# Decode attention and gated MLP block on one Trainium2 core: heads 1 to 14 as a loop on the chip over standing buffers

## The chip, the core and the metric

The kernel runs on one core of a Trainium2 chip. A core has five engines with instruction streams of their own: TensorE (PE, matrix multiply into PSUM), VectorE (DVE), ScalarE (ACT), GpSimd (POOL) and SyncE (SP), which here only issues loads. Sixteen DMA engines move data between HBM and the on-chip memory (SBUF). The engines order each other by semaphores. The metric is the device time of one execution in microseconds; lower is better.

## The reference

One token for each of two batch rows passes a pre-norm attention block with a KV cache and then a bilinear gated MLP. All data are 32-bit floats.

```python
B, Sq, D = 2, 1, 448          # batch, one query token, model width
H, Sk, Dh = 16, 8192, 256     # heads, cached keys, head width; F = 1792
q = (layernorm(x) @ wq).reshape(B, Sq, H, Dh).transpose(0, 2, 1, 3)
scores = einsum("bhqd,bhkd->bhqk", q, k_cache) * Dh ** -0.5
o = einsum("bhqk,bhkd->bhqd", softmax(scores), v_cache)
h = x + o.transpose(0, 2, 1, 3).reshape(B, Sq, H * Dh) @ wo
n = layernorm(h)
out = h + ((n @ w_gate) * (n @ w_up)) @ w_down
```

Each of the 32 pairs of head and batch row reads 8 MB (8192 KB) of K and 8 MB of V once; this is nearly all of the data.

## The kernel before, in words

The work is one Python loop over steps n = 0 to 32 (lines 306 to 343), written out flat in the instruction streams; n counts pairs of head and batch row, h = n // 2, b = n % 2. Step n computes the scores of pair n and the weighted sum over V of pair n - 1, so K of one pair and V of the pair before are loaded together. The order of the instructions on each engine is the order of the code (`manual_schedule`).

A pair's K comes in two chunks of 4096 KB (`load_cache`, line 160): 128 partitions by 32 keys by 256. In `scores` (line 232) VectorE takes half a chunk at a time: a product with the query (line 239) into `prod`, and a reduction over the head width (line 242), so there are four products and four reductions to a pair. `top` (line 246) takes the maximum of each partition and TensorE transposes it. In the next step `softmax` (line 253) runs between the first and the second quarter of the scores, `norm` a quarter later, and `mix` (line 272) has TensorE multiply the probabilities with V, two keys at a time, into `o_ps`. `mixed` (line 283) gathers that into a column, scales it and, when both batch rows of a head are there, multiplies it with `wo` and adds it to `acc_ps`, which stays in PSUM for the whole kernel.

All loads of the cache and the weights are issued by SP, in the order of the code: for each chunk index first K, then V, and behind chunk 0 the weights of that step. SP waits in this order too: a load that must wait for its buffer holds up all that stand behind it. The buffers of the cache are a pool of four (`RING = 4`), handed out in turn to whichever chunk comes next, K or V. Step 0 has no V, so its two K chunks take buffers 0 and 1, and step 1's K and V chunks 0 take buffers 2 and 3; from step 1 on the order K, V, K, V comes round to the same four places. A K buffer is free when the second product over it has ended (line 239), a V buffer when the `mix` matmuls over it have ended (line 278).

The query weights come for two heads at once (`load_wq`, 896 KB, double buffered), one load in four steps; `queries` (line 206) makes four queries in one place, in the second step of an odd head, between the two halves of `mix`. `first_queries` (line 191) makes those of heads 0 and 1. The output weights `wo` come head by head (448 KB).

Behind step 32 come the MLP's three weight loads, which take ring buffers as they come free, the residual add (line 389), the second norm and the projections.

Of the kernel before, what the change touches and what calls it, by code (L numbers as in the profile page):

```python
# [24 lines left out]
RING = 4  # L25
WQ, WO = 3 * 2 * DH + DH, 2 * D
# [17 lines left out]
def tile_decode_block(  # L44
# [23 lines left out]
    ring = ctx.enter_context(tc.tile_pool(name="ring", bufs=RING))  # L68
    wpool = ctx.enter_context(tc.tile_pool(name="wpool", bufs=2))
    qpool = ctx.enter_context(tc.tile_pool(name="qpool", bufs=4))  # L70
    work = ctx.enter_context(tc.tile_pool(name="work", bufs=2))
    ps_q = ctx.enter_context(tc.tile_pool(name="ps_q", bufs=2, space=bass.MemoryType.PSUM))
    ps_s = ctx.enter_context(tc.tile_pool(name="ps_s", bufs=2, space=bass.MemoryType.PSUM))
    ps_1 = ctx.enter_context(tc.tile_pool(name="ps_1", bufs=1, space=bass.MemoryType.PSUM))
# [24 lines left out]
    o_ps = [ps_1.tile([P, 2 * DH], F32, name=f"o_ps{i}") for i in range(2)]  # L99
    for t in o_ps:  # L100
        nc.vector.memset(t, 0.0)  # L101
# [15 lines left out]
    def center(h, tag):  # L117

        mean = ps_s.tile([P, B], F32, tag="sm", name=f"mean_{tag}")
        nc.tensor.matmul(mean, avg, over_chunks(h, f"h_{tag}"), start=True, stop=True)  # L120
# [17 lines left out]
    def transposed(src, tag):  # L138
        ps = ps_s.tile([P, DC, B], F32, tag="sm", name=f"T_ps_{tag}")
        for c in range(DC):  # L140
            nc.tensor.transpose(ps[:, c, :], src[:, c * P : (c + 1) * P], ident[:B, :B])
# [4 lines left out]

    def load_wq(hp):
        t = wpool.tile([P, WQ], F32, tag="wq", name=f"wq_{hp}")
        nc.sync.dma_start(t, wq[hp])
# [4 lines left out]
    def load_wo(h):

        if h % 2 == 0:
            wo_t[h // 2] = wpool.tile([P, 2, WO], F32, tag="wo", name=f"wo_{h // 2}")
        nc.sync.dma_start(wo_t[h // 2][:, h % 2, :], wo[h])

    def load_cache(src, b, h, c, name, parts=(JC,)):  # L160
        t = ring.tile([P, JC, DH], F32, tag="ring", name=f"{name}_{h}_{b}_{c}")
        n = P * JC
        keys = src[b, h, c * n : (c + 1) * n].rearrange("(p j) d -> p j d", p=P)
        at = 0
        for k in parts:
            nc.sync.dma_start(t[:, at : at + k, :], keys[:, at : at + k, :])
# [10 lines left out]
    var = ps_s.tile([P, B], F32, tag="sm", name="var_x")  # L177
# [13 lines left out]
    def first_queries(w):  # L191

        got = [qpool.tile([P, 2, DH], F32, tag="q", name=f"q_0_{b}") for b in range(B)]
        for k in range(2):
            for b in range(B):
                ps = ps_q.tile([P, DH], F32, tag="q", name=f"q_ps_0_{k}_{b}")
                for c in range(DC):
                    at = c * 2 * DH + (k * DH if c < DC - 1 else 0)
                    nc.tensor.matmul(  # L199
                        ps, xb[:, c + (k if c == DC - 1 else 0), b, :], w[:, at : at + DH],  # L200
                        start=(c == 0), stop=(c == DC - 1),
                    )
                nc.scalar.activation(got[b][:, k, :], ps, AF.Copy)
        return got

    def queries(hp, w):

        got = []
        for b in range(B):
            ps = ps_q.tile([P, 2 * DH], F32, tag="q", name=f"q_ps_{hp}_{b}")  # L210
            for c in range(DC - 1):
                nc.tensor.matmul(  # L212
                    ps, xb[:, c, b, :], w[:, c * 2 * DH : (c + 1) * 2 * DH],
                    start=(c == 0), stop=False,
                )
            for k in range(2):
                nc.tensor.matmul(  # L217
                    ps[:, k * DH : (k + 1) * DH], xb[:, DC - 1 + k, b, :],
                    w[:, 3 * 2 * DH : WQ], start=False, stop=(k == 1),
                )  # L220
            q = qpool.tile([P, 2, DH], F32, tag="q", name=f"q_{hp}_{b}")
            nc.scalar.activation(q.rearrange("p h d -> p (h d)"), ps, AF.Copy)  # L222
            got.append(q)
        return got
# [4 lines left out]
    s_t, p_t, rl_t, l_t, mT_t, oT_t = {}, {}, {}, {}, {}, {}
    HC = JC // 2  # L230

    def scores(i, kt, part):
# [6 lines left out]
        nc.vector.tensor_mul(  # L239
            prod, kt[c][:, k * HC : (k + 1) * HC, :], q[:, None, :].to_broadcast([P, HC, DH])  # L240
        )
        nc.vector.tensor_reduce(  # L242
            s_t[i][:, part * HC : (part + 1) * HC], prod, axis=AX.X, op=ALU.add
        )

    def top(i):

        m = work.tile([P, 1], F32, tag="m", name=f"m_{i}")
        nc.vector.tensor_reduce(m, s_t[i], axis=AX.X, op=ALU.max)  # L249
        mT_t[i] = ps_s.tile([1, P], F32, tag="sm", name=f"mT_{i}")  # L250
        nc.tensor.transpose(mT_t[i], m, ident)  # L251

    def softmax(i):
        nm = work.tile([1, 1], F32, tag="nm", name=f"nm_{i}")
        nc.vector.tensor_reduce(nm, mT_t[i], axis=AX.X, op=ALU.max, negate=True)  # L255
        nb_ps = ps_s.tile([P, 1], F32, tag="sm", name=f"nb_ps_{i}")
        nc.tensor.matmul(nb_ps, row, nm, start=True, stop=True)  # L257
        nb = work.tile([P, 1], F32, tag="nb", name=f"nb_{i}")
        nc.scalar.activation(nb, nb_ps, AF.Copy)  # L259
        p_t[i] = work.tile([P, NJ], F32, tag="p", name=f"p_{i}")  # L260
        lsum = work.tile([P, 1], F32, tag="lsum", name=f"lsum_{i}")
# [4 lines left out]
        nc.tensor.matmul(l_t[i], ones, lsum, start=True, stop=True)  # L266

    def norm(i):
        rl_t[i] = work.tile([P, 1], F32, tag="rl", name=f"rl_{i}")
        nc.vector.reciprocal(rl_t[i], l_t[i])  # L270

    def mix(i, vt, c):

        o, p = o_ps[i % 2], p_t[i]
        for t in range(c * JC // 2, (c + 1) * JC // 2):
# [7 lines left out]
    def mixed(i):  # L283

        h, b = divmod(i, B)
        o_sb = work.tile([P, 2 * DH], F32, tag="o_sb", name=f"o_sb_{i}")
        nc.scalar.activation(o_sb, o_ps[i % 2], AF.Copy)  # L287
        oT_ps = ps_s.tile([P, 2], F32, tag="sm", name=f"oT_ps_{i}")
# [8 lines left out]
        nc.scalar.activation(oT_t[h][:, :, b], oT_ps, AF.Copy, scale=rl_t[i])  # L297
        if b == B - 1:
            w = wo_t[h // 2][:, h % 2, :]
            for c in range(2):  # L300
                nc.tensor.matmul(  # L301
                    acc_ps, oT_t[h][:, c, :], w[:, c * D : (c + 1) * D],
                    start=(h == 0 and c == 0), stop=(h == H - 1 and c == 1),
                )

    for n in range(NQ + 1):
        kt, vt = [], []
        hp, at = divmod(n, 2 * B)
        for c in range(NCH):
            if n < NQ:  # L310
                parts = FIRST if n == 0 and c == 0 else (JC,)
                kt.append(load_cache(k_cache, n % B, n // B, c, "k", parts))
            if n > 0:
                parts = LAST if n == NQ and c == NCH - 1 else (JC,)
                vt.append(load_cache(v_cache, (n - 1) % B, (n - 1) // B, c, "v", parts))
            if c == 0 and at == 1:
                load_wo(2 * hp)
            if c == 0 and at == 3 and hp + 1 < H // 2:
                load_wo(2 * hp + 1)
            if c == 0 and at == 2 and hp + 1 < H // 2:  # L320
                w_t[hp + 1] = load_wq(hp + 1)
        if n == NQ:
            load_wo(H - 1)
        if n < NQ:
            scores(n, kt, 0)
        if n > 0:
            softmax(n - 1)
# [175 lines left out]
```

## Time and profile before

| | |
|---|---|
| median of 3 runs | 1314.99 us (1314.83 to 1315.04) |
| the profiled execution's own time | 1314.9 us |
| its span in the profile | 1313.1 us |
| bytes moved | 561.64 MB, mean 428 GB/s |
| instructions | 6974 |
| mean granted TensorE clock | 0.653 of full speed |

The span runs from the first to the last instruction. "Idle before" in a group of instructions is the time its engine stood still just ahead of them, with what ended it. Timeline rows give the start and the length in microseconds, the engine, the line and the operation; `x4` means that four like instructions are merged. `SPq` rows are issues of loads by SP: the length is that of the issue, not of the transfer. A window row gives for each engine the busy time and, in brackets, the number of instructions; the last three numbers are the granted TensorE clock, the busy share of the DMA engines and GB/s. A matmul of 32-bit floats shows as two instructions (two passes), each with a weight load.

### The profile page before, as it was taken

The page shows a single profiled execution, that of the slowest core. Times are in us where ns is not written, and L with a number is a line of the kernel's source. Part 1 is how long each engine was busy: PE and PEld are TensorE (multiplying, and loading weights), DVE is VectorE, ACT ScalarE, POOL GpSimd, SP SyncE. Part 2 cuts the span into 40 slices and gives each one's busy share as a digit, 9 for nine tenths or more (in the row PEclk, how much of TensorE's full clock was granted, in tenths as well). Part 3 has the DMA queues.
Part 4 walks back from the last instruction along what each step waited for, and adds up shares of the span by engine and source line. Part 5 has one row for each costly group of instructions (what it writes and reads, how often), then busy time and mean ns, then how long its engine had stood idle before and what let it go on. Part 6 is the DMA issues. An engine that isn't in the chain of part 4 may idle for free.

```text
span 1313.1 us, 6974 instructions
## 1 busy us (share of the span) xinstructions
PE 569.9 (43%) x2936; PEld 173.4 (13%) x2936; DVE 1153.3 (88%) x395; ACT 60.7 (5%) x183; POOL 1.2 (0%) x8
## 2 busy tenths in 40 slices
PE   3224553354432743426433453524525246254357
PEld 2011110111010210102110021101101002011013
DVE  7999999898998899888998889988998989989971
ACT  1000000000000000000000000000000000000000
POOL 0000000000000000000000000000000000000000
PEclk8556766657765666657666567666676667565668
DMA  9999999999999999999999999999999999999997
GB/s 408 430 430 433 430 432 429 428 433 433 431 428 434 430 431 426 435 429 432 431 431 431 434 429 431 430 425 434 430 431 431 433 428 435 431 430 431 431 424 336
DMA packets 23091, 561.64 MB, mean 428 GB/s; under 512 B 2578, under 2 KB 2580, under 8 KB 5908
## 3 DMA queue, kind: packets, MB, share of 16 engines
q1 hardware_dynamic: 23048, 561.20, 99.6%
q8 instruction: 23, 0.38, 0.1%
q14 instruction: 8, 0.07, 0.0%
q10 hardware_dynamic: 12, 0.01, 0.0%
HBM read 561.19 MB, written 0.00 MB: 427 GB/s over the span
## 4 chain that ended last, share of the span: by engine, by line
DMA 79%; PE 14%; DVE 5%; issue 1%; ACT 0%; POOLq 0%; SPq 0%; POOL 0%
DMA v<-in_A_v_cache_dram 77%; PE o_ps L278 13%; DVE prod L239 3%; DMA wu_t<-in_B_w_up_dram 2%; DVE s L242 2%; PE q_ps L199 0%; PE u_ps L379 0%; PE y_ps L438 0%; DVE o_ps L101 0%; PE hm_ps L431 0%; PE oT_ps L291 0%; ACT o_sb L287 0%; PE mean_x L120 0%; DVE xb L134 0%; PE var_x L178 0%
## 5 line engine op out<-in xcount | busy, mean ns | idle before, releaser
L239 DVE TENSOR_TENSOR prod<-k,q 128x4096 f32<-128x4096 f32 x128 | 565.7, 4420 | 115.6 <-DMA k<-in_A_k_cache_dram 110.7
L242 DVE TENSOR_REDUCE s<-prod 128x16 f32<-128x4096 f32 x128 | 565.8, 4420 | 6.0
L278 PE MATMUL o_ps<-v,p 128*2 128x512 f32 x2048 | 371.3, 891 | 338.1 <-DMA v<-in_A_v_cache_dram 338.1
L278 PEld LDWEIGHTS o_ps<-v,p 128*2 128x2 f32 x2048 | 59.2, 109 | 613.6 <-DMA v<-in_A_v_cache_dram 367.3
L257 PE MATMUL nb_ps<-nm,row 1*128 1x1 f32 x64 | 17.9, 347 | 280.0 <-DVE nm L255 280.0
L257 PEld LDWEIGHTS nb_ps<-nm,row 1*128 1x128 f32 x64 | 15.7, 303 | 287.2 <-issue 158.7
L287 ACT ACTIVATE o_sb<-o_ps 128x512 f32<-128x512 f32 x32 | 19.1, 597 | 679.2 <-PE o_ps L278 679.2
L301 PE MATMUL acc_ps<-wo,oT 128*2 128x448 f32 x64 | 43.9, 834 | 5.6 <-ACT oT L297 5.6
L291 PE MATMUL oT_ps<-sel,o_sb 128*128 128x1 f32 x256 | 33.7, 253 | 23.2 <-ACT o_sb L287 23.2
L212 PE MATMUL q_ps<-wq,xb 128*128 128x512 f32 x84 | 39.1, 601 | 0.0
L291 PEld LDWEIGHTS oT_ps<-sel,o_sb 128*128 128x128 f32 x256 | 31.0, 191 | 55.9 <-ACT o_sb L287 55.9
L251 PE MATMUL mT<-ident,m 128*1 128x128 f32 x32 | 10.2, 318 | 61.2 <-DVE m L249 60.9
L266 PE MATMUL l_ps<-lsum,ones 128*128 128x1 f32 x64 | 18.7, 362 | 23.5 <-ACT p L262 23.5
L259 ACT ACTIVATE nb<-nb_ps 128x1 f32<-128x1 f32 x32 | 5.5, 171 | 406.8 <-PE nb_ps L257 406.8
L266 PEld LDWEIGHTS l_ps<-lsum,ones 128*128 128x128 f32 x64 | 16.0, 310 | 26.2 <-ACT p L262 26.2
L212 PEld LDWEIGHTS q_ps<-wq,xb 128*128 128x128 f32 x84 | 15.4, 190 | 20.6 <-issue 20.3
L217 PE MATMUL q_ps<-wq,xb 128*128 128x256 f32 x56 | 14.4, 379 | 0.0
L251 PEld LDWEIGHTS mT<-ident,m 128*1 128x1 f32 x32 | 2.5, 79 | 84.7 <-issue 50.0
L389 DVE TENSOR_TENSOR h_sb<-x_sb,acc_ps 2x448 f32<-2x448 f32 x1 | 0.6, 609 | 13.8 <-PE acc_ps L301 13.8
L222 ACT ACTIVATE q<-q_ps 128x512 f32<-128x512 f32 x14 | 8.4, 597 | 92.1 <-PE q_ps L217 92.1
L217 PEld LDWEIGHTS q_ps<-wq,xb 128*128 128x128 f32 x56 | 10.6, 190 | 7.4 <-issue 6.7
L262 ACT ACTIVATE p<-s,nb 128x64 f32<-128x64 f32 x32 | 11.1, 348 | 1.0
(79 smaller groups left out, 101.8 us busy)
## 6 DMA issues: line engine op xcount, KB each, us to landing
k<-in_A_k_cache_dram SPq DMA_DIRECT2D x63, 4096.0 KB, 26.5
v<-in_A_v_cache_dram SPq DMA_DIRECT2D x63, 4096.0 KB, 33.2
wq<-in_wq_dram SPq DMA_DIRECT2D x8, 896.0 KB, 34.6
wo<-in_wo_dram SPq DMA_DIRECT2D x16, 448.0 KB, 33.5
k<-in_A_k_cache_dram SPq DMA_DIRECT2D x2, 2048.0 KB, 13.5
wg_t<-in_B_w_gate_dram SPq DMA_DIRECT2D x1, 3136.0 KB, 24.5
wu_t<-in_B_w_up_dram SPq DMA_DIRECT2D x1, 3136.0 KB, 30.4
v<-in_A_v_cache_dram SPq DMA_DIRECT2D x1, 2048.0 KB
```

The source lines that it names most:

```text
L212: nc.tensor.matmul(ps, xb[:, c, b, :], w[:, c * 2 * DH : (c + 1) * 2 * DH], start=(c == 0), stop=False,)
L217: nc.tensor.matmul(ps[:, k * DH : (k + 1) * DH], xb[:, DC - 1 + k, b, :], w[:, 3 * 2 * DH : WQ], start=False, stop=(k == 1),)
L239: nc.vector.tensor_mul(prod, kt[c][:, k * HC : (k + 1) * HC, :], q[:, None, :].to_broadcast([P, HC, DH]))
L242: nc.vector.tensor_reduce(s_t[i][:, part * HC : (part + 1) * HC], prod, axis=AX.X, op=ALU.add)
L251: nc.tensor.transpose(mT_t[i], m, ident)
L257: nc.tensor.matmul(nb_ps, row, nm, start=True, stop=True)
L262: nc.scalar.activation(p_t[i], s_t[i], AF.Exp, bias=nb, scale=DH**-0.5, accum_out=lsum)
L266: nc.tensor.matmul(l_t[i], ones, lsum, start=True, stop=True)
L278: nc.tensor.matmul(o[g : g + 2, :], p[:, 2 * t : 2 * t + 2], vt[c][:, j : j + 2, :], start=(t < 4), stop=(t >= NJ // 2 - 4),)
L287: nc.scalar.activation(o_sb, o_ps[i % 2], AF.Copy)
L291: nc.tensor.matmul(oT_ps[:, c : c + 1], o_sb[:, (2 * k + c) * P : (2 * k + c + 1) * P], sel[:, k : k + 1], start=(k == 0), stop=(k == 1),)
L301: nc.tensor.matmul(acc_ps, oT_t[h][:, c, :], w[:, c * D : (c + 1) * D], start=(h == 0 and c == 0), stop=(h == H - 1 and c == 1),)
```

## The change

- Steps are now grouped by head in a function `query_steps(h, first, more)`, which holds the two steps b = 0 and b = 1 of one head. It is called flat for head 0 and for head 15; heads 1 to 14 are one loop on the chip, `tc.For_i(1, H - 1, ...)`, whose body is traced once. Loads take their address from the loop variable.
[...]
- All pools but one for constants and one for PSUM are gone. K chunk c always goes to `k_sb[c]`, V chunk c to `v_sb[c]`; the small tiles, `wq_sb` and `wo_sb` stand once each, queries, scores and probabilities once for each batch row.
- Query weights come head by head (448 KB, 16 loads), in the step b = 1 before they are needed, and `query` makes the next head's two queries between the halves of `mix`. Its last 64 rows of D are packed as two 128-wide halves in place of two heads.
- The residual x is put into `acc_ps` by a matmul with the identity ahead of the first query, and copies take the place of the adds behind it.
- The MLP's weights go to `k_sb[0]`, `k_sb[1]` and `v_sb[0]`.

```diff
-RING = 4
-WQ, WO = 3 * 2 * DH + DH, 2 * D
+HD = DH // 2
+HINT = (mybir.EngineType.PE,)
+WQ, WO = 3 * DH + DH // 2, 2 * D
...
+    k_sb = [const.tile([P, JC, DH], F32, name=f"k_sb{c}") for c in range(NCH)]
+    v_sb = [const.tile([P, JC, DH], F32, name=f"v_sb{c}") for c in range(NCH)]
+    wq_sb = const.tile([P, WQ], F32, name="wq_sb")
+    wo_sb = const.tile([P, WO], F32, name="wo_sb")
+    q_sb = [const.tile([P, DH], F32, name=f"q_sb{b}") for b in range(B)]
...
+    def load_cache(dst, src, b, h, c, parts=(JC,)):
         n = P * JC
-        keys = src[b, h, c * n : (c + 1) * n].rearrange("(p j) d -> p j d", p=P)
+        keys = src[b, bass.ds(h, 1), c * n : (c + 1) * n].rearrange("o (p j) d -> p (o j) d", p=P)
...
+    nc.tensor.matmul(acc_ps, ident[:B, :B], x_sb[:, :D], start=True, stop=False)
...
+    def query(b):
+        for c in range(DC - 1):
+            nc.tensor.matmul(
+                q_ps[b][:, :DH], xb[:, c, b, :], wq_sb[:, c * DH : (c + 1) * DH],
+                start=(c == 0), stop=False,
+            )
         for k in range(2):
...
+            nc.tensor.matmul(
+                q_ps[b][:, k * HD : (k + 1) * HD], xb[:, DC - 1 + k, b, :], wq_sb[:, 3 * DH :],
+                start=False, stop=(k == 1),
+            )
...
+    def query_steps(h, first, more):
+        for b in range(B):
+            before = b > 0 or not first
+            for c in range(NCH):
+                load_cache(k_sb[c], k_cache, b, h, c, FIRST if first and b == c == 0 else (JC,))
+                if before:
+                    load_cache(v_sb[c], v_cache, 1 - b, h if b else h - 1, c)
+                if c == 0 and b == 0 and before:
+                    load_w(wo_sb, wo, h - 1)
+                if c == 0 and b == 1 and more:
+                    load_w(wq_sb, wq, h + 1)
+            scores(b, 0)
+            if before:
+                softmax(1 - b)
+            scores(b, 1)
+            if before:
+                norm()
             for part in range(2, 2 * NCH):
+                scores(b, part)
+            for c in range(NCH):
+                if c > 0 and b == 1 and more:
+                    query(0)
+                    query(1)
+                    take_query(0)
+                if before:
+                    mix(1 - b, c)
+            if before:
+                mixed(1 - b)
+            top(b)
+            if b == 1 and more:
+                take_query(1)
+
+    for b in range(B):
+        query(b)
+        take_query(b)
+    query_steps(0, True, True)
+    with tc.For_i(1, H - 1, 1, name="heads", iteration_sync="reg_based",
+                  hint_engines=HINT, head_align_engines=(mybir.EngineType.PE,)) as i:
+        query_steps(i, False, True)
+    query_steps(H - 1, False, False)
+    for c in range(NCH):
+        load_cache(v_sb[c], v_cache, B - 1, H - 1, c, LAST if c == NCH - 1 else (JC,))
+    load_w(wo_sb, wo, H - 1)
+    softmax(1)
...
+    mixed(1, last=True)
...
-    nc.vector.tensor_add(h_sb[:, :D], x_sb[:, :D], acc_ps)
+    nc.vector.tensor_copy(h_sb[:, :D], acc_ps)
```

More of the change, by code (lines that the diff above doesn't have):

```diff
@@ L67, in tile_decode_block @@
     const = ctx.enter_context(tc.tile_pool(name="const", bufs=1))
[L68 to L74, printed above, removed]
+    psum = ctx.enter_context(tc.tile_pool(name="psum", bufs=1, space=bass.MemoryType.PSUM))
     x_sb = const.tile([B, DC * P], F32, name="x_sb")
@@ L98, in tile_decode_block @@
     )
-    o_ps = [ps_1.tile([P, 2 * DH], F32, name=f"o_ps{i}") for i in range(2)]
+    o_ps = [psum.tile([P, 2 * DH], F32, name=f"o_ps{i}") for i in range(2)]
     for t in o_ps:
         nc.vector.memset(t, 0.0)
-    acc_ps = ps_1.tile([B, D], F32, name="acc_ps")
-    y_ps = ps_1.tile([P, YW], F32, name="y_ps")
+    acc_ps = psum.tile([B, D], F32, name="acc_ps")
+    y_ps = psum.tile([P, YW], F32, name="y_ps")
     nc.vector.memset(y_ps, 0.0)
+    q_ps = [psum.tile([P, 2 * DH], F32, name=f"q_ps{b}") for b in range(B)]
+    sm_ps = [psum.tile([P, 2 * DH], F32, name=f"sm_ps{i}") for i in range(2)]
+    k_sb = [const.tile([P, JC, DH], F32, name=f"k_sb{c}") for c in range(NCH)]
[3 more added lines that the diff above has]
+    q_sb = [const.tile([P, DH], F32, name=f"q_sb{b}") for b in range(B)]
+    s_sb = [const.tile([P, NJ], F32, name=f"s_sb{b}") for b in range(B)]
+    p_sb = [const.tile([P, NJ], F32, name=f"p_sb{b}") for b in range(B)]
+    m_sb = const.tile([P, 1], F32, name="m_sb")
+    nm_sb = const.tile([1, 1], F32, name="nm_sb")
+    nb_sb = const.tile([P, 1], F32, name="nb_sb")
+    lsum_sb = const.tile([P, 1], F32, name="lsum_sb")
+    rl_sb = const.tile([P, 1], F32, name="rl_sb")
+    o_sb = const.tile([P, 2 * DH], F32, name="o_sb")
+    oT_sb = const.tile([P, 2, B], F32, name="oT_sb")
     def over_chunks(t, tag):
@@ L117, in center @@
     def center(h, tag):
-        mean = ps_s.tile([P, B], F32, tag="sm", name=f"mean_{tag}")
+        mean = sm_ps[1][:, :B]
         nc.tensor.matmul(mean, avg, over_chunks(h, f"h_{tag}"), start=True, stop=True)
@@ L176, in tile_decode_block @@
     xc = center(xT, "x")
-    var = ps_s.tile([P, B], F32, tag="sm", name="var_x")
+    var = sm_ps[0][:, :B]
     nc.tensor.matmul(var, avg, squares(xc, "x"), start=True, stop=True)
@@ L206, in queries @@
[L206 to L224, printed above, removed]
@@ L244, in scores, with top @@
         )
[L246 to L261, printed above, removed]
+    def top(b):
+        nc.vector.tensor_reduce(m_sb, s_sb[b], axis=AX.X, op=ALU.max)
+        nc.tensor.transpose(sm_ps[0][:1, :P], m_sb, ident)
@@ L262, in softmax @@
+    def softmax(b):
+        nc.vector.tensor_reduce(nm_sb, sm_ps[0][:1, :P], axis=AX.X, op=ALU.max, negate=True)
+        nb_ps = sm_ps[1][:, 0:1]
+        nc.tensor.matmul(nb_ps, row, nm_sb, start=True, stop=True)
+        nc.scalar.activation(nb_sb, nb_ps, AF.Copy)
         nc.scalar.activation(
-            p_t[i], s_t[i], AF.Exp, bias=nb, scale=DH**-0.5, accum_out=lsum
+            p_sb[b], s_sb[b], AF.Exp, bias=nb_sb, scale=DH**-0.5, accum_out=lsum_sb
         )
-        l_t[i] = ps_s.tile([P, 1], F32, tag="sm", name=f"l_ps_{i}")
@@ L266, in softmax, with norm, mix @@
[L266 to L274, printed above, removed]
+        nc.tensor.matmul(sm_ps[1][:, 1:2], ones, lsum_sb, start=True, stop=True)
+    def norm():
+        nc.vector.reciprocal(rl_sb, sm_ps[1][:, 1:2])
+    def mix(b, c):
         for t in range(c * JC // 2, (c + 1) * JC // 2):
@@ L278, in mix, with mixed @@
             nc.tensor.matmul(
-                o[g : g + 2, :], p[:, 2 * t : 2 * t + 2], vt[c][:, j : j + 2, :],
+                o_ps[b][g : g + 2, :], p_sb[b][:, 2 * t : 2 * t + 2], v_sb[c][:, j : j + 2, :],
                 start=(t < 4), stop=(t >= NJ // 2 - 4),
             )
[L283 to L288, printed above, removed]
+    def mixed(b, last=False):
+        nc.scalar.activation(o_sb, o_ps[b], AF.Copy)
+        oT_ps = sm_ps[1][:, 2:4]
         for c in range(2):
@@ L294, in mixed @@
                 )
-        if b == 0:
-            oT_t[h] = work.tile([P, 2, B], F32, tag="oT", name=f"oT_{h}")
-        nc.scalar.activation(oT_t[h][:, :, b], oT_ps, AF.Copy, scale=rl_t[i])
+        nc.scalar.activation(oT_sb[:, :, b], oT_ps, AF.Copy, scale=rl_sb)
         if b == B - 1:
-            w = wo_t[h // 2][:, h % 2, :]
             for c in range(2):
                 nc.tensor.matmul(
-                    acc_ps, oT_t[h][:, c, :], w[:, c * D : (c + 1) * D],
-                    start=(h == 0 and c == 0), stop=(h == H - 1 and c == 1),
-                )
@@ L306, in tile_decode_block @@
[L306 to L327, printed above, removed]
-        if n < NQ:
-            scores(n, kt, 1)
-        if n > 0:
-            norm(n - 1)
-        if n < NQ:
-            for part in range(2, 2 * NCH):
-                scores(n, kt, part)
-        for c in range(NCH):
-            if c > 0 and at == 3 and hp + 1 < H // 2:
-                q_t[hp + 1] = queries(hp + 1, w_t[hp + 1])
-            if n > 0:
-                mix(n - 1, vt, c)
-        if n > 0:
-            mixed(n - 1)
-        if n < NQ:
-            top(n)
@@ L346, in load_ff @@
-    def load_ff(w, name):
-        t = ring.tile([P, NF * D], F32, tag="ring", name=name)
+                    acc_ps, oT_sb[:, c, :], wo_sb[:, c * D : (c + 1) * D],
+                    start=False, stop=(last and c == 1),
+                )
+    def query_steps(h, first, more):
[15 more added lines that the diff above has]
+                norm()
+            for part in range(2, 2 * NCH):
+                scores(b, part)
[11 more added lines that the diff above has]
+                take_query(1)
@@ L348, in load_ff @@
+    for c in range(NCH):
+        mix(1, c)
+    mixed(1, last=True)
+    def load_ff(t, w):
+        t = t.rearrange("p j d -> p (j d)")[:, : NF * D]
         nc.sync.dma_start(t, w)
         return t
-    wg_t = load_ff(wg, "wg_t")
-    wu_t = load_ff(wu, "wu_t")
-    wd_t = ring.tile([P, NF, D], F32, tag="ring", name="wd_t")
+    wg_t = load_ff(k_sb[0], wg)
+    wu_t = load_ff(k_sb[1], wu)
+    wd_t = v_sb[0].rearrange("p j d -> p (j d)")[:, : NF * D].rearrange("p (n d) -> p n d", d=D)
     at = 0
@@ L419, in tile_decode_block @@
         if k == 0:
-            u_ps.append(ps_q.tile([P, FH], F32, tag="q", name="u_ps0"))
+            u_ps.append(q_ps[1][:, :FH])
         else:
-            u_ps.append(blank("u_ps1", FH))
+            u_ps.append(blank(q_ps[0], FH))
         project(u_ps[k], wu_t, k * FH, (k + 1) * FH)
@@ L456, in pack @@
     wq, wo = np.asarray(inputs["A_wq"]), np.asarray(inputs["A_wo"])
-    n = 2 * DH
     rows = []
-    for hp in range(H // 2):
-        a = wq[:, hp * n : (hp + 1) * n]
-        top = a[: 3 * P].reshape(3, P, n).transpose(1, 0, 2).reshape(P, 3 * n)
-        last = np.concatenate([a[3 * P :, :DH], a[3 * P :, DH:]], axis=0)
+    for h in range(H):
+        a = wq[:, h * DH : (h + 1) * DH]
+        top = a[: 3 * P].reshape(3, P, DH).transpose(1, 0, 2).reshape(P, 3 * DH)
+        last = np.concatenate([a[3 * P :, :HD], a[3 * P :, HD:]], axis=0)
         rows.append(np.concatenate([top, last], axis=1))
```

62 lines of the change are left out of this document (18 added, 44 removed).

## The prediction

> **What bounds the kernel now.** I read the page's busy shares first, then the DMA rows, then the chain that ended last.
>
> ```profile
> PE 569.9 (43%) x2936; PEld 173.4 (13%) x2936; DVE 1153.3 (88%) x395; ACT 60.7 (5%) x183; POOL 1.2 (0%) x8
> ...
> GB/s 408 430 430 433 430 432 429 428 433 433 431 428 434 430 431 426 435 429 432 431 431 431 434 429 431 430 425 434 430 431 431 433 428 435 431 430 431 431 424 336
> ...
> q8 instruction: 23, 0.38, 0.1%
> ...
> DMA v<-in_A_v_cache_dram 77%; PE o_ps L278 13%; DVE prod L239 3%; DMA wu_t<-in_B_w_up_dram 2%; DVE s L242 2%; PE q_ps L199 0%; PE u_ps L379 0%; PE y_ps L438 0%; DVE o_ps L101 0%; PE hm_ps L431 0%; PE oT_ps L291 0%; ACT o_sb L287 0%; PE mean_x L120 0%; DVE xb L134 0%; PE var_x L178 0%
> ...
> L239 DVE TENSOR_TENSOR prod<-k,q 128x4096 f32<-128x4096 f32 x128 | 565.7, 4420 | 115.6 <-DMA k<-in_A_k_cache_dram 110.7
> L278 PE MATMUL o_ps<-v,p 128*2 128x512 f32 x2048 | 371.3, 891 | 338.1 <-DMA v<-in_A_v_cache_dram 338.1
> ```
>
> The flat row of GB/s says it: the transfers run at some 430 GB/s from start to end and never pause. VectorE, 88% busy, still waits for K (110.7 us), and TensorE waits for V (338.1 us). So the time is the bytes over the rate, and an edit costs only if it leaves the transfer engines with nothing queued. That idle time is lost for good, since nothing can move faster later. I therefore ask of each edit when SyncE (SP) can issue the next load, and when the bytes already queued run out. The first rows of SP, and those that set them:
>
> ```profile
> 0.73 0.39 SPq L149 DMA_DIRECT2D wq<-in_wq_dram  x1
> 1.19 2.35 SPq L166 DMA_DIRECT2D k<-in_A_k_cache_dram  x4
> 3.58 0.52 SPq L166 DMA_DIRECT2D v<-in_A_v_cache_dram  x1
> ...
> 7.28 10.12 PE L199 MATMUL q_ps<-wq,xb 128*128 128x256 f32 x32 [1.35 <-DVE xb L134]
> ...
> 11.09 0.38 ACT L203 ACTIVATE q<-q_ps 128x256 f32<-128x256 f32 x1 [3.35 <-PE q_ps L199]
> 11.51 4.42 DVE L239 TENSOR_TENSOR prod<-k,q 128x4096 f32<-128x4096 f32 x1 [3.77 <-ACT q L203]
> ...
> 24.87 0.33 SPq L166 DMA_DIRECT2D k<-in_A_k_cache_dram  x1
> ...
> 42.70 0.33 SPq L166 DMA_DIRECT2D v<-in_A_v_cache_dram  x1
> ...
> 60.71 0.33 SPq L166 DMA_DIRECT2D k<-in_A_k_cache_dram  x1
> ```
> ```profile
> 78.54 0.33 SPq L166 DMA_DIRECT2D k<-in_A_k_cache_dram  x1
> ```
> ```profile
> 0.00:5.00 5.00, 1.30 (x6) 1.07 (x6) 2.73 (x15) 1.28 (x1) 1.25 (x8) 1.00 0.70 269
> 5.00:10.00 5.00, 3.28 (x9) 2.69 (x10) 1.56 (x7) 1.75 (x3) 0.00 (x0) 1.00 0.98 416
> 10.00:20.00 10.00, 7.39 (x27) 5.92 (x25) 8.46 (x2) 1.53 (x4) 0.00 (x0) 1.00 1.02 437
> 20.00:30.00 10.00, 0.00 (x0) 0.00 (x0) 9.90 (x4) 0.00 (x0) 0.00 (x0) 0.50 1.02 442
> ```
>
> The x4 row is K(0) chunk 0 in two parts, K(0) chunk 1 and K(1) chunk 0; V(0) chunk 0 follows. All four ring buffers are filled at once. The first reuse is at 24.87, when the second product over K(0) chunk 0 ends, 13.36 us after the first product began at 11.51. The last column of the stretches is GB/s: 269 over 5 us is 1.35 MB, 3.13 us at 430, so bytes flow from 1.87, 1.14 us after SP began the first issue.
>
> **The change part by part.** *Standing buffers, at the start.* K has two buffers of its own, so K(1) chunk 0 must wait for buffer 0, and behind that wait in SP's order stand V(0) chunk 0, wq(1), K(1) chunk 1 and V(0) chunk 1. Queued ahead are one wq of 0.46 MB and two chunks of 4.19 MB: 8.85 MB. The stretches give 1.35 + 2.08 + 4.37 = 7.80 MB by 20.0, and the other 1.05 MB at 442 takes 2.4 us: dry at 22.4. The first product: the query of one batch row was eight 256-wide passes (the row's x32 is four queries), from 7.28 to the copy at 11.09, 0.48 us each. Now it is six of them and four 128-wide ones, for which the nearest row is 301 ns (a 128x128 transpose, quoted below): 2.9 + 1.2 = 4.1 in place of 3.8, 0.3 us more. The matmul that puts x into acc_ps stands ahead of it, two passes of 834 ns, 1.67 us in a gap of 1.35: 0.3 us more. So the first product starts near 12.0, the buffer is free at 25.4, bytes flow at 26.5: **4.1 us idle** (3.2 to 4.9 for a start between 11.1 and 12.8). VectorE itself runs 0.5 us later than before.
>
> ```profile
> L301 PE MATMUL acc_ps<-wo,oT 128*2 128x448 f32 x64 | 43.9, 834 | 5.6 <-ACT oT L297 5.6
> L212 PE MATMUL q_ps<-wq,xb 128*128 128x512 f32 x84 | 39.1, 601 | 0.0
> ...
> L217 PE MATMUL q_ps<-wq,xb 128*128 128x256 f32 x56 | 14.4, 379 | 0.0
> ...
> L431 PE MATMUL hm_ps<-ident,hm 128*128 128x128 f32 x4 | 0.9, 301 | 0.6 <-DVE hm L428 0.6
> ```
>
> *In the middle of the loop* the ring had fallen into the same order (K0, V0, K1, V1 each into its old place), so the buffers cost nothing there. The rows of one step with queries, K chunk 1 arriving at 457.44 and V chunk 1 at 467.10 (the one before it at 427.13):
>
> ```profile
> 427.13 6.56 PE L278 MATMUL o_ps<-v,p 128*2 128x512 f32 x32 [13.81 <-DMA v<-in_A_v_cache_dram]
> ```
> ```profile
> 450.31 0.33 SPq L166 DMA_DIRECT2D k<-in_A_k_cache_dram  x1
> ...
> 457.44 4.42 DVE L239 TENSOR_TENSOR prod<-k,q 128x4096 f32<-128x4096 f32 x1 [2.63 <-DMA k<-in_A_k_cache_dram]
> ...
> 467.10 5.35 PE L278 MATMUL o_ps<-v,p 128*2 128x512 f32 x32 [5.74 <-DMA v<-in_A_v_cache_dram]
> 470.81 0.33 SPq L166 DMA_DIRECT2D k<-in_A_k_cache_dram  x1
> ...
> 475.27 0.22 DVE L249 TENSOR_REDUCE m<-s 128x1 f32<-128x64 f32 x1
> 475.54 0.08 PEld L251 LDWEIGHTS mT<-ident,m 128*1 128x1 f32 x1 [1.40 <-DVE m L249]
> 475.54 0.27 PE L251 MATMUL mT<-ident,m 128*1 128x128 f32 x1 [1.31 <-DVE m L249]
> 476.86 4.42 DVE L239 TENSOR_TENSOR prod<-k,q 128x4096 f32<-128x4096 f32 x1 [1.37 <-DMA k<-in_A_k_cache_dram]
> ```
>
> K of the next step is issued at 450.31 while bytes are queued until 467.10: SP may be 15 us late without cost (16.8 less 1.14). Branches, register steps and longer issues on SP lie in that cover; without it a microsecond each would be 14 us. Queries per head: 12 passes of 256 and 8 of 128 are 12 x 379 + 8 x 301 = 7.0 us (379 ns: the 256-wide passes of L217) where a pair took 12 x 601 + 8 x 379 = 10.2 us; both fit before V chunk 1, where TensorE had 5.74 us left. Weights head by head keep the bytes: 16 loads of 448 KB for 8 of 896. Their rows are as long as wo's now, and with a wo among them loads go at the full rate: 427.13 to 467.10 is 39.97 us for four chunks and a wo, 17.24 MB at 431 GB/s. The single wq and wo buffers were last read a step or more before SP comes to them. I take 0 (at most 0.9 us off, if all instruction packets went: q8's 0.38 MB at 430 GB/s).
>
> *The loop's two ends.* An instruction of the body serves fourteen passes, and its wait must mean the same in each. What the first pass needs from head 0, and what head 15 needs from the last pass, is in other code, so I expect those waits gathered at the ends, ahead of and behind the loop. No row shows this; I bound it.
>
> At entry: bytes flow from 26.5, and K(1) chunk 0, V(0) chunk 0, wq(1), K(1) chunk 1, V(0) chunk 1 are 17.24 MB, 40.0 us at 431: dry at 66.5. If the body's first load waits for its own buffer alone, that comes near 61 (before: the K row at 60.71) and the entry costs 0. If SP waits at the entry for all four buffers, the last is K buffer 1: 78.54 plus 0.5 is 79.0, flow at 80.2: **13.7 us**. If all engines must have arrived, VectorE's reduce and maximum (4.42 + 0.22), the transpose (0.3) and a meeting of engines (0.7, row below) come on top: 19.4 us. Nothing below 0 can come, since bytes don't go faster. I take 13.7: it asks only that SP knows its own buffers free before the loop, and no meeting of engines.
>
> At exit, head 15's first K is behind all work of the last pass. Queued bytes end with V chunk 1 (467.10 in the step shown), all engines end at 475.81 (transpose), 8.7 us later; with 0.7 for a meeting and 1.14 to flow that is **10.5 us**. Were only VectorE's last product waited for (470.81), 4.8; exact waits, 0; dearer meeting, some 13. I take 10.5, since the work behind a loop can name only the loop as a whole.
>
> ```profile
> SPq L487 <- PEq L487: 0.7, 1, 0.7
> ```
>
> [...]
>
> *The tail.* V(31) chunk 1 now waits for the second V buffer, not for the first:
>
> ```profile
> 1266.05 5.24 PE L278 MATMUL o_ps<-v,p 128*2 128x512 f32 x32 [12.36 <-DMA v<-in_A_v_cache_dram]
> ...
> 1271.36 0.33 SPq L348 DMA_DIRECT2D wu_t<-in_B_w_up_dram  x1
> ```
>
> It can be issued at 1271.36 and flow at 1272.5, while V(31) chunk 0, 9.7 us behind the landing at 1266.05, lasts until 1275.8: 3.3 us of cover, 0 cost. wg, wu and wd follow in the same order. The copy of acc_ps replaces an add of the same shape: 0.
>
> Sum, on the profiled execution's own 1314.9 us (span 1313.1, 1.8 around it; the median of runs, 1314.99, is 0.1 above): 1314.9 + 4.1 + 13.7 + 10.5 = **1343.2**.
>
> **Rivals.** (a) The exit stops SP, the entry doesn't: for it speaks that SP could name head 0's instructions exactly: 1314.9 + 4.1 + 10.5 = 1329.5. (b) Neither stops, or the loop is laid out flat again: 1319.0. (c) The buffers' waits inside the loop name whole passes: SP would issue at 475.8 what it issued at 450.31, bytes dry at 467.10, 10 us or so in each of 13 back edges: 1343.2 + 130 = 1473. [...] (d) Back edges stall on fetching code. VectorE idles 2.63 + 1.37 us in the step shown, some 8 us a head, so a stall under 8 us is regained and each microsecond above it costs 13; at 10 us, 1343.2 + 26 = 1369. The nearest rows, the small load of x and its first user, have 1.5 us, which would cost 0:
>
> ```profile
> 0.74 0.55 ACTq L78 DMA_DIRECT2D x_sb<-in_A_x_dram  x1
> ...
> 2.26 0.45 PE L141 MATMUL T_ps_x<-ident,x_sb 2*128 2x2 f32 x3 [2.26 <-DMA x_sb<-in_A_x_dram]
> ```
>
> [...]
>
> (e) Not slower: the start gap is covered. The place is SP's wait for K buffer 0, the price 4.1; it decides if the first product starts by 10.5 (gap under 2.6), with both ends free: 1317. Against: xb alone keeps TensorE until 7.28.
>
> **How the numbers follow.** Runs spread by 0.2 us; I call 0.2%, 2.6 us, the least that tells. Both ends stop 0.56 (1339 to 1351); (a) 0.26; (b) 0.06; (c) 0.04; (d) 0.03; (e) 0.05. The time is that of the likeliest, 1343.2. The range takes in both ends stopping with all engines meeting (1314.9 + 4.1 + 19.4 + 13 = 1351, some microseconds added) and (a) down to the cheap exit (1323.8); left out are (b) to (e), 0.18. Slower by over 0.2% are the cases but (e): 0.93 with a little of it; no change 0.05; faster, 0.02, if the instruction bytes saved were worth more than all stops.
>
> **What would show it.** SP's issue of K(1) chunk 0 near 25.4 and a dip in the first number of GB/s; SP's next K, of head 1, near 79 (right) or 61 (a); SP's K of head 15 some 8 to 10 us after the last V chunk of the loop landed, with VectorE idle about 10 us more there; between them the rate flat at 430 and waits for K as before. Wrong: a dip in every head (c, d), or none at either end (b).

## The result and the profile after

The changed kernel takes 1347.81 us (median of 5, 1347.58 to 1348.16) against 1315.04 us for the kernel before (median of 5): 32.8 us slower, a ratio of 1.025 (95% interval 1.0236 to 1.0264). Its profiled execution took 1348.11 us, with a span of 1346.3 us.

From its page: GB/s in 40 slices, the packets of the instruction queue, and the two large groups.

```profile
GB/s 356 419 210 429 430 433 434 428 428 433 433 431 427 429 428 440 429 426 433 433 432 428 430 433 434 428 428 433 433 430 430 427 434 425 438 335 356 434 422 350
...
q8 instruction: 7, 0.11, 0.0%
...
L218 DVE TENSOR_TENSOR prod<-k_sb,q_sb 128x4096 f32<-128x4096 f32 x128 | 565.7, 4420 | 148.3 <-DMA k_sb<-in_A_k_cache_dram 143.2
L221 DVE TENSOR_REDUCE s_sb<-prod 128x16 f32<-128x4096 f32 x128 | 565.8, 4420 | 5.4
L248 PE MATMUL o_ps<-v_sb,p_sb 128*2 128x512 f32 x2048 | 364.0, 875 | 350.1 <-DMA v_sb<-in_A_v_cache_dram 350.1
```

The row that was flat has three holes: at the start (356), in the third slice (210), and in slices 36 and 37 (335, 356). VectorE's work is the same to 0.1 us; it only waits 32.5 us more for K. Stretches of the changed kernel and, below them, the same of the kernel before (last columns: granted TensorE clock, busy share of the DMA engines, GB/s):

```profile
0.00:28.00 28.00, 9.75 (x30) 6.87 (x30) 20.56 (x25) 3.80 (x6) 1.25 (x8) 0.79 0.84 341
...
60.00:90.00 30.00, 13.37 (x89) 5.76 (x81) 23.18 (x8) 1.63 (x4) 0.00 (x0) 0.67 0.40 163
90.00:1200.00 1110.00, 464.09 (x2451) 156.04 (x2451) 986.19 (x304) 49.34 (x165) 0.00 (x0) 0.67 1.00 431
1200.00:1225.00 25.00, 6.79 (x41) 1.94 (x41) 15.28 (x5) 1.14 (x3) 0.00 (x0) 0.65 0.48 197
```
```profile
0.00:28.00 28.00, 11.97 (x40) 9.68 (x40) 20.68 (x25) 4.56 (x8) 1.25 (x8) 0.86 0.95 404
...
60.00:90.00 30.00, 8.26 (x69) 2.26 (x61) 29.73 (x10) 0.86 (x2) 0.00 (x0) 0.67 1.00 425
90.00:1200.00 1110.00, 486.51 (x2352) 140.10 (x2352) 996.51 (x308) 49.55 (x154) 0.00 (x0) 0.65 1.00 431
1200.00:1225.00 25.00, 7.45 (x36) 1.99 (x36) 23.33 (x8) 0.61 (x3) 0.00 (x0) 0.57 1.00 428
```

The missing bytes over 431 GB/s: start (404 - 341) x 28 / 431 = 4.1 us, loop entry (425 - 163) x 30 / 431 = 18.2 us, loop exit (428 - 197) x 25 / 431 = 13.4 us. In the 1110 us between, nearly all of the fourteen passes, the rate is 431 in both. The holes make 35.7 us, 2.9 more than the measured 32.8; the last section comes back to that.

What SP waited for at the two ends (L308 is the line of the loop), and the rows around the entry:

```profile
SPq L167 <- DVEq L308: 38.3, 1, 38.3
SPq L308 <- DMA v_sb<-in_A_v_cache_dram: 33.6, 1, 33.6
...
SPq L308 <- DVE m_sb L227: 8.4, 1, 8.4
SPq L333 <- PE o_ps L248: 5.8, 2, 4.4
...
SPq L308 <- PE sm_ps L228: 0.3, 1, 0.3
```
```profile
43.20 0.44 SPq L167 DMA_DIRECT2D v_sb<-in_A_v_cache_dram  x1
```
```profile
83.13 0.22 DVE L227 TENSOR_REDUCE m_sb<-s_sb 128x1 f32<-128x64 f32 x1
83.37 0.35 SPq L167 DMA_DIRECT2D k_sb<-in_A_k_cache_dram  x1
83.40 0.08 PEld L228 LDWEIGHTS sm_ps<-ident,m_sb 128*1 128x1 f32 x1 [9.77 <-DVE m_sb L227]
83.40 0.37 PE L228 MATMUL sm_ps<-ident,m_sb 128*1 128x128 f32 x1 [9.69 <-DVE m_sb L227]
84.08 0.34 SPq L167 DMA_DIRECT2D v_sb<-in_A_v_cache_dram  x1
```

SP issued the last load of head 0 at 43.20 and the first of the loop at 83.37, 0.02 us after VectorE had ended its last instruction ahead of the loop (83.13 + 0.22); the wait is put down to VectorE's own queue at the loop's line. It did not wait for TensorE there: the transpose began only at 83.40. V, which TensorE frees, came at 84.08, behind that transpose. The three L308 rows are the exit: SP waited 33.6 us for the loop's last V to land, then 8.4 us for VectorE's last maximum and 0.3 us for TensorE's last transpose.

### The profile page after: what moved, and what is told of

The parts are those of the page before. It is cut to its first block, busy times and chain, and to the rows that moved or that the text cites. A ratio compares the mean times of both kernels' runs of the same rounds, so it can differ in the third digit from the quotient of the medians.

```text
span 1346.3 us, 8499 instructions
## 1 busy us (share of the span) xinstructions
PE 556.4 (41%) x3086; PEld 191.3 (14%) x3086; DVE 1153.6 (86%) x395; ACT 61.6 (5%) x197; POOL 1.2 (0%) x8
## 5 line engine op out<-in xcount | busy, mean ns | idle before, releaser
L218 DVE TENSOR_TENSOR prod<-k_sb,q_sb 128x4096 f32<-128x4096 f32 x128 | 565.7, 4420 | 148.3 <-DMA k_sb<-in_A_k_cache_dram 143.2
L221 DVE TENSOR_REDUCE s_sb<-prod 128x16 f32<-128x4096 f32 x128 | 565.8, 4420 | 5.4
L248 PE MATMUL o_ps<-v_sb,p_sb 128*2 128x512 f32 x2048 | 364.0, 875 | 350.1 <-DMA v_sb<-in_A_v_cache_dram 350.1
L248 PEld LDWEIGHTS o_ps<-v_sb,p_sb 128*2 128x2 f32 x2048 | 58.3, 108 | 612.7 <-DMA v_sb<-in_A_v_cache_dram 370.1
L202 PE MATMUL q_ps<-wq_sb,xb 128*128 128x256 f32 x192 | 50.6, 402 | 0.0
L259 PE MATMUL sm_ps<-sel,o_sb 128*128 128x1 f32 x256 | 33.7, 253 | 26.3 <-ACT o_sb L255 26.3
L259 PEld LDWEIGHTS sm_ps<-sel,o_sb 128*128 128x128 f32 x256 | 31.0, 191 | 57.7 <-ACT o_sb L255 57.7
L202 PEld LDWEIGHTS q_ps<-wq_sb,xb 128*128 128x128 f32 x192 | 35.4, 198 | 19.3 <-issue 14.0
L266 PE MATMUL acc_ps<-wo_sb,oT_sb 128*2 128x448 f32 x64 | 35.3, 687 | 5.7 <-ACT oT_sb L263 5.7
L207 PEld LDWEIGHTS q_ps<-wq_sb,xb 128*128 128x128 f32 x128 | 19.8, 196 | 1.8
L207 PE MATMUL q_ps<-wq_sb,xb 128*128 128x128 f32 x128 | 19.9, 279 | 0.0
L213 ACT ACTIVATE q_sb<-q_ps 128x256 f32<-128x256 f32 x32 | 12.2, 381 | 135.6 <-PE q_ps L207 130.9
L365 DVE COPY h_sb<-acc_ps 2x448 f32<-2x448 f32 x1 | 0.6, 612 | 13.4 <-PE acc_ps L266 13.4
## 6 DMA issues: line engine op xcount, KB each, us to landing
k_sb<-in_A_k_cache_dram SPq DMA_DIRECT2D x2, 2048.0 KB, 10.5
```

The lines of the kernel that those rows point to most:

```text
L202: nc.tensor.matmul(q_ps[b][:, :DH], xb[:, c, b, :], wq_sb[:, c * DH : (c + 1) * DH], start=(c == 0), stop=False,)
L207: nc.tensor.matmul(q_ps[b][:, k * HD : (k + 1) * HD], xb[:, DC - 1 + k, b, :], wq_sb[:, 3 * DH :], start=False, stop=(k == 1),)
L213: nc.scalar.activation(q_sb[b], q_ps[b][:, :DH], AF.Copy)
L218: nc.vector.tensor_mul(prod, k_sb[c][:, k * HC : (k + 1) * HC, :], q_sb[b][:, None, :].to_broadcast([P, HC, DH]))
L221: nc.vector.tensor_reduce(s_sb[b][:, part * HC : (part + 1) * HC], prod, axis=AX.X, op=ALU.add)
L248: nc.tensor.matmul(o_ps[b][g : g + 2, :], p_sb[b][:, 2 * t : 2 * t + 2], v_sb[c][:, j : j + 2, :], start=(t < 4), stop=(t >= NJ // 2 - 4),)
```

## The experiments

Each ratio is against runs of the kernel before taken beside it (medians 1315.2 to 1315.5 us); differences in microseconds are between the medians given here.

**Where the cost sits: e1 to e4.** They edit only which heads the loop covers.

```diff
 e1  -    with tc.For_i(1, H - 1, 1, ...) as i:        +    for i in range(1, H - 1):
 e2  -    with tc.For_i(1, H - 1, 1, ...) as i:        +    with tc.For_i(1, 3, 1, ...) as i:   # heads 3 to 14 flat behind it
 e3  -    with tc.For_i(1, H - 1, 1, ...) as i:        +    For_i(1, 8, 1, ...), then For_i(8, H - 1, 1, ...)
 e4       query_steps(0, True, True)                   +    query_steps(1, False, True)
     -    with tc.For_i(1, H - 1, 1, ...) as i:        +    with tc.For_i(2, H - 1, 1, ...) as i:
```

> Heads 1 to 14 written out flat, all else as in the changed kernel (standing buffers, weights head by head, x in acc_ps). If the two ends of the loop cost 18 and 13 us (dips of the changed kernel's GB/s at 60 to 90 and 1200 to 1225 us), only the start gap of some 4 us is left: 1317 to 1320. If the cost lies in the standing buffers or the smaller weight loads, it stays above 1335.

Measured: 1319.61 us, ratio 1.0033 (1.002 to 1.0045). The loop itself costs 28.2 us; standing buffers, smaller weight loads and x in acc_ps together some 4 us.

> The loop covers heads 1 and 2 alone, heads 3 to 14 are flat. Price at the two ends: 1346 to 1349, as with fourteen passes. Price of each pass (32 us over 14 passes, 2.3 us each): two passes, some 1323.

Measured: 1350.97 us, ratio 1.027 (1.0253 to 1.0287), 2 us above the expected range. Two passes cost as much as fourteen, and 3.2 us more; the last section comes back to these 3.2. The price is one for each loop, not for each pass.

> Heads 1 to 7 and heads 8 to 14 are two loops, one behind the other. Price at the ends: one more stop of 13 us, at which exit and entry fall together: 1360 to 1363. Price of each pass: no change, 1348 or a little less (one jump back less).

Measured: 1362.86 us, ratio 1.0358 (1.0341 to 1.0375): 15.0 us for one more pair of ends, where 1360 to 1363 stands for 12.2 to 15.2. The stretch around the seam:

```profile
640.00:670.00 30.00, 7.67 (x41) 2.05 (x41) 16.26 (x5) 1.14 (x3) 0.00 (x0) 0.61 0.52 213
```

(431 - 213) x 30 / 431 = 15.2 us of bytes missing, the whole of it.

> Heads 0 and 1 flat, the loop covers heads 2 to 14. If SP waits at the entry until VectorE has come there, the price is how far VectorE is behind the last byte: late by its start at 11.6 us in the changed kernel (18 us), but back in step with the loads a head later, some 12 us; the start gap of 4 us is as before: 1340 to 1343. If the entry is a fixed price, 1348. Price of each pass: 1345.5.

Measured: 1341.97 us, ratio 1.0201 (1.0184 to 1.0218): 5.8 us better than the changed kernel. Its entry:

```profile
140.00:180.00 40.00, 8.50 (x49) 2.85 (x47) 25.93 (x7) 1.13 (x3) 0.00 (x0) 0.59 0.72 302
```

```profile
157.20 0.22 DVE L227 TENSOR_REDUCE m_sb<-s_sb 128x1 f32<-128x64 f32 x1
157.44 0.35 SPq L167 DMA_DIRECT2D k_sb<-in_A_k_cache_dram  x1
```

(431 - 302) x 40 / 431 = 12.0 us in place of 18.2. So the entry has no fixed price. Here too SP's first load of the loop comes 0.02 us after VectorE's last instruction ahead of it (157.20 + 0.22): SP waits until VectorE has come to the loop, and the price is how far VectorE is behind the last byte.

**Is the start gap a term of its own: e5, e6.**

```diff
             for c in range(NCH):
+                if before and first:
+                    load_cache(v_sb[c], v_cache, 1 - b, h if b else h - 1, c)
                 load_cache(k_sb[c], k_cache, b, h, c, ...)
-                if before:
+                if before and not first:
                     load_cache(v_sb[c], v_cache, 1 - b, h if b else h - 1, c)
```

> In the step b = 1 of head 0 alone, each V chunk is loaded ahead of the K chunk of its place, so SP has V loads to issue before it waits for K buffer 0; the start gap is covered. If the loop's restart is set by VectorE's arrival at the entry (83.4 us, after two steps of work from its start at 11.6 on), the bytes run dry 4 us earlier there and nothing is won: 1346.5 to 1348.5. If start gap and entry stop are sums of their own, as the prediction had them: 1343.5 to 1344.5.

Measured: 1348.03 us, ratio 1.0247 (1.0232 to 1.0263): no change. Its stretches show why:

```profile
0.00:28.00 28.00, 9.29 (x30) 6.61 (x30) 20.16 (x25) 3.80 (x6) 1.25 (x8) 0.79 0.96 406
...
60.00:90.00 30.00, 13.57 (x89) 5.72 (x81) 23.68 (x8) 1.63 (x4) 0.00 (x0) 0.73 0.27 106
```

The start is whole again (406 against 404 before), and the entry has grown from 18.2 to (425 - 106) x 30 / 431 = 22.2 us. SP's first load of the loop is again put down to VectorE's own queue at the loop's line (38.8 us of waiting, 38.3 in the changed kernel) and is out at 84.23 (43.33 + 40.90, two issues in one row), so 4 us won ahead of it are waited out there.

> The flat version of e1 with the same order of loads in head 0. The start gap, which is all that e1 has left over before, goes: 1315 to 1316, the time of before. If e1's 4 us come from something else (weights, x in acc_ps), it stays at 1319 to 1320.

Measured: 1316.61 us, ratio 1.0009 (1.000 to 1.0018). Without the loop the same edit wins 3.0 us. The flat version is then 1.4 us above the kernel before, 0.6 above the expected range.

**Bytes queued across the ends: e7 to e9.**

```diff
 e7           for c in range(NCH):
+                if c == 0 and b == 0 and before:
+                    continue                       # loaded at the end of the head before
...
             if b == 1 and more:
                 take_query(1)
+                load_cache(k_sb[0], k_cache, 0, h + 1, 0)
+                load_cache(v_sb[0], v_cache, 1, h, 0)
+                load_w(wo_sb, wo, h)
 e8  e7 with the edit of e5
 e9  e8 with
     def load_w(dst, src, h):
-        nc.sync.dma_start(...)
+        nc.gpsimd.dma_start(...)                   # but for the first wq and the last wo
```

> The loop's boundary is moved against the loads: K chunk 0, V chunk 0 and wo of the next head are issued at the end of a pass (and of head 0), not at the head of the next one; the order of loads on SP is unchanged. At the entry 20 us of bytes are then queued when SP waits for VectorE, so the entry costs nothing. At the exit SP waits for everything, the queued loads too: the time from the last byte to its landing seen (2.8 us), the meeting (0.9) and the restart (0.7) stay, some 4.4. From e1: 1319.6 + 4.4, 1322 to 1326. If the stops are a fixed price of a loop, 1348.

Measured: 1342.59 us, ratio 1.0206 (1.019 to 1.0221): 18 us worse than expected. At the ends the edit did what it should (60 to 90 us: 423 GB/s; 1200 to 1230: 417). The loss had moved inside the loop:

```profile
90.00:1150.00 1060.00, 441.91 (x2322) 148.29 (x2326) 936.23 (x289) 47.41 (x159) 0.00 (x0) 0.67 0.99 422
```
```profile
SPq L167 <- DMA v_sb<-in_A_v_cache_dram: 423.1, 15, 32.0
...
SPq L167 <- DMA wo_sb<-in_wo_dram: 5.4, 13, 0.4
```
```profile
137.83 0.33 SPq L171 DMA_DIRECT2D wo_sb<-in_wo_dram  x1
169.06 0.34 SPq L167 DMA_DIRECT2D k_sb<-in_A_k_cache_dram  x1
170.12 0.33 SPq L167 DMA_DIRECT2D v_sb<-in_A_v_cache_dram  x1
```

(431 - 422) x 1060 / 431 = 22 us, 1.6 to 1.7 for each pass. SP stood still from 137.83 to 169.06. Then the first load of the new pass came when V chunk 0, the last but one load of the old pass, had landed, and the second one 1.06 us later, when wo, the very last, had. Nothing was queued by then. I had read the changed kernel's flat rate as a sign that each load waits only for its own buffer; these two waited for landings in other buffers. In the changed kernel itself the same two waits stand at the head of a pass, under cover:

```profile
157.76 4.42 DVE L218 TENSOR_TENSOR prod<-k_sb,q_sb 128x4096 f32<-128x4096 f32 x1 [2.57 <-DMA k_sb<-in_A_k_cache_dram]
157.88 0.33 SPq L167 DMA_DIRECT2D k_sb<-in_A_k_cache_dram  x1
...
167.43 6.43 PE L248 MATMUL o_ps<-v_sb,p_sb 128*2 128x512 f32 x32 [9.70 <-DMA v_sb<-in_A_v_cache_dram]
167.59 0.33 SPq L167 DMA_DIRECT2D v_sb<-in_A_v_cache_dram  x1
```

K chunk 0 of the next head goes 0.12 us after K chunk 1 of the last step has landed, V chunk 0 0.16 us after V chunk 1 has: here too the last two loads of the pass. While V is waited for, K is queued, and no byte is missing.

> e7 with e5's order of loads in head 0. The start gap goes (4 us); the bytes queued at the entry end at some 82.5 us against a restart at 84.1, which gives 1.6 back: 1320 to 1323.

Measured: 1340.21 us, ratio 1.019 (1.0174 to 1.0205), 17 us above the expected range, since e7's loss in each pass stays. Against e7 the edit wins 2.4 us: the start gap of 4 less 1.6, which the entry gives back, as expected (60 to 90 us: 400 GB/s where e7 has 423).

> e8 with the weight loads of head 0, the loop and head 15 but the first wq and the last wo issued by GpSimd, so that a pass has eight loads on SP and not ten. In e7 and e8 the first two loads of a pass waited until the last two of the pass before had landed, V chunk 0 and wo, with nothing else queued: 1.7 us lost in each pass. If that goes with eight loads, what stays over e6 (1316.6) is 1.6 us at the entry and some 4.4 at the exit, less up to 2.8 us of late landings that only flat code shows: 1319 to 1323. If the loss in each pass comes from jumping back or from the loads' moved place, it stays at 1340.

Measured: 1319.45 us, ratio 1.0033 (1.0021 to 1.0046). With eight loads on SP in a pass the waits at its head are gone (SP waits 20.6 us for landings of V, in e8 420.4), and 20.8 us with them. What is left shows at the two ends:

```profile
60.00:90.00 30.00, 13.88 (x93) 5.77 (x81) 28.71 (x10) 1.63 (x4) 0.54 (x1) 0.67 0.97 404
90.00:1200.00 1110.00, 470.78 (x2492) 158.15 (x2492) 996.38 (x307) 50.44 (x168) 14.48 (x27) 0.67 1.00 431
1200.00:1225.00 25.00, 6.00 (x28) 1.84 (x32) 15.88 (x5) 0.61 (x3) 0.00 (x0) 0.50 0.82 339
```

1.5 us at the entry (425 - 404), 5.2 at the exit (428 - 339). At the exit SP's next load comes only at 1209.00, though the engines' last work in the loop ends at 1197.3: SP's waits at the loop's end are put down to landings of V (19.3 us, two waits), so I read it that the loads queued across the exit are waited for there. VectorE, whose K was issued at 1171.63, also starts again only at 1209.05. It is the best loop I found, and still 4.2 us above the kernel before. Why the waits come with ten loads (e7, e8) and not with eight is not shown: other numbers were not tried, and with the number e9 also changes which loads SP issues.

**The arguments of the loop: e10, e11.**

```diff
 e10 -    hint_engines=HINT, head_align_engines=(mybir.EngineType.PE,)
     +    hint_engines=()
 e11 -    iteration_sync="reg_based"
     +    iteration_sync="barrier"
```

> The changed kernel without the branch hint and without the alignment of TensorE's code. TensorE waits 22 us for VectorE behind every jump back at most and some 9 us at least, so a stall there is covered: 1347 to 1348.5. If jumps back cost time on the path, above 1351.

Measured: 1347.7 us, ratio 1.0248 (1.0231 to 1.0265). `hint_engines` and `head_align_engines`, taken out together, change nothing here (1347.81 us with them).

> The changed kernel with iteration_sync barrier: every jump back stops all engines. Each is then a stop like the one between the two loops of e3 (15 us more): 1347.8 + 13 x 14 to 15, 1525 to 1545. [...] If a stop inside a loop were cheaper than at its ends (no loads to wait for), 1400.

Measured: 1494.47 us, ratio 1.1362 (1.1343 to 1.1381): 146.7 us more, 11.3 for each of 13 jumps back, below the 14 to 15 that I took from e3, so the time lies 30 us under the expected range. SP waits at the loop's line 14 times for VectorE's last maximum (116.5 us), in the changed kernel once (8.4 us). So `reg_based` spares 146.7 us here against `barrier`.

## Why the prediction was right, and where its terms were off

The time, 1347.8 us, lies in the range and in the likeliest case, both ends stop; the forecast of 1343.2 is 4.6 short. By its steps:

- *What bounds the kernel.* Right. Bytes over rate set the time, and the changed work of the engines had no effect of its own that shows: e1, which has the new query groups and the copies, is some 4 us above the kernel before, as much as the start gap.
- *Start, 4.1 us.* The size was right: K(1) chunk 0 was issued near 25 us, the first product began at 11.63 and not 12.0, and 4.1 us of bytes are missing. It belongs in the sum of the holes, but it is no saving that stands by itself, and the forecast's own times say so: with the restart at 80.2 fixed, bytes that flow 4.1 us earlier run dry 4.1 us earlier and the entry grows by as much. e5 shows it; its expectation of 1343.5 to 1344.5 "as the prediction had them" misread that sum.
- *Entry, 13.7 us.* The step that failed in size. I took the case that SP waits for its own buffers (79.0), with no meeting of engines; it waited until VectorE had come to the loop (83.37), with 18.2 us measured, 4.5 above the term. That is near the dearer bound of 19.4, but not by its mechanism, since SP did not wait for TensorE. e4 fits: 12.0 us where VectorE is in step with the loads. Why the wait names VectorE's arrival and not its last product over K buffer 1 stays open.
- *Exit, 10.5 us.* The mechanism was right, the term 2.9 us short. I let the queued bytes end when V chunk 1 is seen to land; the flow falls off earlier:

```profile
1200.00:1204.00 4.00, 0.00 (x0) 0.00 (x0) 3.97 (x2) 0.00 (x0) 0.00 (x0) 0.57 0.99 426
1204.00:1205.00 1.00, 0.00 (x0) 0.00 (x0) 1.00 (x1) 0.00 (x0) 0.00 (x0) 0.50 0.16 66
1205.00:1206.00 1.00, 0.00 (x0) 0.00 (x0) 1.00 (x1) 0.00 (x0) 0.00 (x0) 0.50 0.08 33
1206.00:1207.00 1.00, 0.00 (x0) 0.00 (x0) 0.97 (x2) 0.00 (x0) 0.00 (x0) 0.50 0.00 0
...
1217.00:1218.00 1.00, 0.00 (x0) 0.00 (x0) 0.00 (x0) 0.00 (x0) 0.00 (x0) 0.81 1.46 410
```
```profile
1207.02 5.47 PE L248 MATMUL o_ps<-v_sb,p_sb 128*2 128x512 f32 x32 [8.95 <-DMA v_sb<-in_A_v_cache_dram]
...
1215.47 0.27 PE L228 MATMUL sm_ps<-ident,m_sb 128*1 128x128 f32 x1 [1.13 <-DVE m_sb L227]
1216.35 0.34 SPq L167 DMA_DIRECT2D k_sb<-in_A_k_cache_dram  x1
```

The flow falls off at 1204, TensorE sees the landing at 1207.02, the last transpose ends at 1215.74, SP issues at 1216.35 and bytes flow again near 1217. So some 2.8 us of landing, 8.7 of work (as predicted), 0.6 for the meeting and 0.7 to flow: 12.8 of the 13.4. The 2.8 are mostly the end of the stream and not a wait behind its last byte. The rows count a packet's bytes where it starts (1205.20 to 1205.24 has 819 GB/s, what follows up to 1207 has 0); the last packet of data, 32 KB, starts there and takes 1.2 us (0.08 of 16 engines for 1 us), so it ends near 1206.5, and TensorE starts some 0.6 us later. What was short in my sum was the end of the stream and the entry.
- *Middle, 0.* Right, by the rate of 431 in both. The cover that I named for SP, 15 us, is smaller than I said, since the first two loads of a pass wait for the last two landings (from K's issue at 157.88 to V's landing at 167.43 it is 9.5 us); e7 shows what happens where it is gone.
- *Rival (c), waits inside the loop.* Partly there, in the first two loads of a pass, without a cost in the changed kernel (431 GB/s). *Rival (d), fetching code.* Not seen: without `hint_engines` and `head_align_engines` (e10) the time is the same, 1347.7 us. The trace shows no packet of instructions at the jumps back: instruction queue q8 has 7 packets in all against 23, and neither it nor the other instruction queue (q14) has one between 100 and 1160 us, where the kernel before has 18 and 7.
- *Rivals (a), (b), (e).* None came; e1 is (b) made on purpose, 1319.61 for a forecast of 1319.0.
- *How near the number came.* Partly luck. The entry was 4.5 us short and the exit 2.9, 7.4 together; the time is only 4.6 over the forecast because the kernel before loses some 2.8 us inside that the changed kernel does not (last section), which I had not seen. A slip without weight: the cases but (e) have 0.95 together, where I wrote 0.93.

## What to carry to other kernels

In this kernel, which lives on a full load queue, the loop on the chip cost at its two ends (18.2 and 13.4 us) and not at its jumps back. In one like it, ask how many bytes are queued when the issuing engine has to wait there, and who is the last to arrive. Give the loop a boundary at which loads are in flight (e7 to e9), and then look at what the first loads of a pass wait for: with ten loads by SP in a pass, the first two waited for the last two to land. The gap at the start, ahead of an entry whose end VectorE set, cost nothing more, and closing it won nothing (e5: 1348.03 us against 1347.81).

## What the runs showed of the hardware beyond the forecast

Two things. At the exit the flow of the last chunk falls off some 2.8 us before its reader starts, of which 0.6 lie behind its last packet; in the full stream, at 431 GB/s, this does not show, and at the stop it is paid. And flat code has late landings that the loop's inside has not. In the steady pattern K chunks come 19.4 us apart, and 20.55 where a load of 448 KB of weights lies between. Of the kernel before:

```profile
515.71 4.43 DVE L239 TENSOR_TENSOR prod<-k,q 128x4096 f32<-128x4096 f32 x1 [1.38 <-DMA k<-in_A_k_cache_dram]
536.27 4.42 DVE L239 TENSOR_TENSOR prod<-k,q 128x4096 f32<-128x4096 f32 x1 [2.56 <-DMA k<-in_A_k_cache_dram]
557.05 4.42 DVE L239 TENSOR_TENSOR prod<-k,q 128x4096 f32<-128x4096 f32 x1 [2.74 <-DMA k<-in_A_k_cache_dram]
```

557.05 is 1.4 us late (20.78 where 19.4 is due). The kernel before has two such steps, 2.8 us together; e2, flat from head 3 on, has four, 3.4 us together, leaving out the step right behind its exit; the inside of the changed kernel's loop has none in 1100 us. That brings the sum to 4.1 + 18.2 + 13.4 - 2.8 = 32.9, measured 32.8, and would account for e2's 3.2 us over the changed kernel. Both are sums over one profile each, and no run takes the late landings away by themselves. The late steps go with flat code, for which the kernel before moves 25 packets of instructions between 100 and 1160 us and the changed kernel none. That these make the steps is not shown: most of the 25 have no late step beside them.
